# Three chunks of a retention kernel turned by transposing DMAs from ScalarE's queue instead of TensorE's and SyncE's

## The chip, the cores and the metric

One core of a Trainium2 chip. The time is the device time of one execution in microseconds; several runs are summed up by their median. All times inside an execution are counted from its first instruction.

## The reference

Two layers. The first is retention (attention with a decay in place of a softmax) on `q`, `k`, `v` of shape 8 x 8 x 576 x 64 (batch, heads, sequence, head size); its output, 4608 x 512, goes through a gated feed-forward layer.

```
scores = q @ k.T / sqrt(64)
gamma  = 1 - 2 ** (-5 - head)
ret    = scores * (gamma ** (i - j) where i >= j, else 0)
x      = (ret @ v), heads side by side        # 4608 x 512
out    = (sigmoid(x @ w_gate) * (x @ w_val)) @ w_out    # 512 -> 1536 -> 512
```

## The kernel before

The sequence of a batch is cut into chunks of 128 tokens. Inside a chunk the scores are computed in full; between chunks a running state per head (the sum of k times v) is carried. The decay is split into factors for q and for k, so that a cast to bf16 and a multiplication by a table are one operation. The first chunks are done in pairs at the start (`PAIRS`); the other thirty, called "later chunks" here and numbered 0 to 29 in the list `STEPS`, are done while the feed-forward layer of earlier tokens runs. The feed-forward layer takes tokens in blocks (`BLOCKS`): block 0 of the main loop has 256 tokens and begins at token 512, then one more of 256, then blocks of 512.

For a later chunk s there are these steps:

- `load(s)`: three loads from HBM (`k_s`, `q_s`, `v_s`), given out on SP's queue (L171);
- `cast_qk`: k and q times their tables into `natural_qk[s]` (`qk` in the profile, L429), on GpSimd, for chunks 0 and 1 q on VectorE; `cast_v` (L444);
- the turning: `T` holds q and k with the head size on the partitions. Either `turn_step(s)` does it by eight TensorE transposes into PSUM (L630) and one copy each by ScalarE and VectorE (L632), for the chunks in `TURNED`, or `cross(s)` does it by one transposing DMA from SBUF to SBUF (L448), given out on SP's queue right behind the casts;
- `slot_of_two`: scores (`row`, L686) that read `T`, products for the state (`new`, L695), the mask (L704) and the values (`val`, L718 and L734).

`casts_to(s)` does the loads, casts and `cross` of all chunks up to s that are still to be done; its loads run one or two chunks ahead of its casts.

In block 0 of the main loop `h_units` goes through twelve units on TensorE, alternately `h_g` (gate, two columns of 128 out of 1536) and `h_v` (value). Each fills one of three PSUM banks that rotate (`ffn_psum`). ScalarE takes `h_g` out by a sigmoid into `gv` (L889), VectorE multiplies `h_v` into it (L891). The table `SUMS_AT` says what further work is written behind which unit: an entry such as `0.6:t01p` stands for block 0, unit 6, `turn_step(1)`, `0.0:c03p` for `casts_to(3)`. The scores of chunks 0 and 1 stand behind unit 10, those of chunks 2 and 3 in the next slot. Every engine runs its instructions in the order in which they are written.

Just ahead of the main loop the first 512 tokens go through the output matmul, `op_first` (L1549): `FIRST_OP_CUTS` counts how many of its 512-wide matmuls are split into two of 256.

The completion of a DMA is counted by one of eight counters, `DMAHW0` to `DMAHW7`, that are handed out in turn. A DMA waits until the one that had its counter before it has landed.

Of the kernel before, what the change touches and what calls it, by code (L numbers as in the profile page):

```python
# [16 lines left out]
def kernel(  # L17
# [19 lines left out]
    nc = tc.nc  # L37
# [109 lines left out]
    def half(x):  # L147
        return slice(x * 64, x * 64 + 64)
# [169 lines left out]
    def wo_sums(i, part, parts, eng=nc.vector):  # L318

        fp = slice(part * (NFC // 2) // parts, (part + 1) * (NFC // 2) // parts)  # L320
        b11, b12, b21, b22 = (wo_sb[:, r::2, c:c + DM // 2][:, fp] for r in range(2) for c in (0, DM // 2))
        t1, t2, t4 = (wt_sb[:, j, fp] for j in range(3))
        to, a, b = ((t1, b12, b11), (t2, b22, t1), (b12, b22, b12), (t4, b21, t2))[i]
        eng.tensor_tensor(out=to, in0=a, in1=b, op=ALU.subtract)
# [34 lines left out]
    def w_sums(kind, i, u, eng):  # L359

        a11, a12, a21, a22 = w_quarters(kind, u)
        s1, s2, s4 = (wt3_sb[kind][j][u] for j in range(3))
        to, a, b, op = ((s1, a21, a22, ALU.add), (s2, s1, a11, ALU.subtract), (seventh(kind, u), a11, a21, ALU.subtract),
                        (s4, a12, s2, ALU.subtract))[i]
        eng.tensor_tensor(out=to, in0=a, in1=b, op=op)
# [54 lines left out]
    def cast_qk(s, i, eng):  # L420
        c = STEPS[s][1]
        if i == 1:
            natural_qk[s] = nat_pool.tile([P, 2, M, P], BF16, tag="qk", name=f"qk_{s}")
        to = natural_qk[s][:, i].rearrange("p m (y d) -> p y m d", y=2)
        if i == 1 and s >= SCALED_V:
            (on_pool if s in K_ON_POOL else on_act)(out=to, in_=by_halves(loaded[s][0]))
            return
        tab = (qtab, ktab)[i][:, c, :].rearrange("p (y m) -> p y m", y=2).unsqueeze(3).to_broadcast([P, 2, M, D])
        eng.tensor_tensor(out=to, in0=by_halves(loaded[s][1 - i]), in1=tab, op=ALU.mult)  # L429
# [8 lines left out]
    def cast_v(s, eng):  # L438
        natural["v", s] = nat_pool.tile([P, H, D], BF16, tag="v", name=f"v_{s}", bufs=6)
        if s >= SCALED_V:  # L440
            tab = ktab[:, STEPS[s][1], :].unsqueeze(2).to_broadcast([P, H, D])
            nc.gpsimd.tensor_tensor(out=natural["v", s], in0=loaded[s][2], in1=tab, op=ALU.mult)  # L442
        else:
            eng(out=natural["v", s], in_=loaded[s][2])  # L444

    def cross(s):
        t = att_pool.tile([P, 2, M, P], BF16, tag="T", name=f"T_{s}", bufs=6)
        nc.sync.dma_start_transpose(out=t.rearrange("p j m t -> p (j m) t"),  # L448
                                    in_=natural_qk[s].rearrange("p j m d -> p (j m d)"))
        turned[s] = t  # L450

# [167 lines left out]
            cols = slice(t0, t0 + P)  # L619
            eng(out=x_out(slice(i * k, (i + 1) * k), cols), in_=x_in(ps[:, at_m:at_m + k], cols))  # L620

    TURNED = (0, 1, 7)

    def turn_step(s):

        t = att_pool.tile([P, 2, M, P], BF16, tag="T", name=f"T_{s}", bufs=6)
        for i, ((pool, tag), eng) in enumerate(zip(VALS, (on_act, on_dve))):
            ps = pool.tile([P, M, P], BF16, tag=tag, name=f"turn_{s}_{i}")
            for m in range(M):
                nc.tensor.matmul(ps[:, m, :], lhsT=natural_qk[s][:, i, m, :], rhs=ident, is_transpose=True,  # L630
                                 start=(m == 0), stop=(m == M - 1))
            eng(out=t[:, i], in_=ps)  # L632
        turned[s] = t
# [6 lines left out]
    def new_state(key, dt=BF16):  # L640
        b, c, j = key
        if dt == BF16 and c == LAST - 1 and j == NJ - 1:
            return nat_pool.tile([P, M, D], dt, tag="sf", name=f"sf_{b}_{c}_{j}", bufs=5)
        tag, bufs = ("s32", 3) if dt == FP32 else ("sb", 4)
        if (tag, b, c) not in both_steps:
            both_steps[tag, b, c] = nat_pool.tile([P, NJ, M, D], dt, tag=tag, name=f"{tag}_{b}_{c}", bufs=bufs)
        return both_steps[tag, b, c][:, j]
# [142 lines left out]
    def after_two(vals, news, i, late, first, closes):  # L790

        if i == 0 and not news:
            for s in vals:
                inter(s, [(1,), (0,)])
        if i < NJ:
            if len(vals) == 2 and at_col[vals[1]] == at_col[vals[0]] + P:
                leave_two(vals, i)
            else:
                for s in vals:
                    nc.scalar.copy(out=x_out(ALL, cols_of(s, i)), in_=x_in(val_ps[s][i], cols_of(s, i)))  # L800
        if i == NJ:
            for s in vals:
                if dealt(cols_of(s, 0)):
                    x_sums(at_col[s], X_LATE if late and closes else X_FIRST)
        if late and news and i == (NJ if closes else NJ - 1):
            casts_to(min(done["cast"], news[-1] + LEAD_CAST + 1) if first and not closes else news[-1] + LEAD_CAST + 1)
        for n, s in enumerate(news):
            b, c = STEPS[s]
            if c == LAST:
                continue  # L810
            if i == n:
                add_state(s, 0)
                add_state(s, 1)
                if s < 2 * len(PAIRS_AT) and s == max(x for x in news if STEPS[x][1] < LAST):
                    ffn_psum.free_last(ffn_psum.held.pop())
            if i == n + 1:
                keep_both(b, c, [j for j in range(NJ) if totals.pop((s, j), None) is not None], on_act)
# [16 lines left out]
    def first_batch_state():  # L834

        whole = new_state((0, LAST - 1, NJ - 1))
        for hh in range(2):
            for y in range(2):
                (nc.vector.tensor_copy if hh == y else nc.sync.dma_start)(
                    out=whole[half(y), hh::2, :], in_=sbd[3][half(hh), 2 * y:2 * y + 2, half(hh)])  # L840
        state[0, LAST - 1, NJ - 1] = whole
# [6 lines left out]
    def loads_to(s):  # L848
        while done["ld"] <= min(NS - 1, s):
            load(done["ld"])  # L850
            done["ld"] += 1

    def casts_to(s):
        while done["cast"] <= min(NS - 1, s):
            x = done["cast"]
            loads_to(x + (AHEAD[x] if x < len(AHEAD) else 2))
            cast_qk(x, 1, nc.gpsimd)
            cast_qk(x, 0, nc.vector if x < 2 else nc.gpsimd)
            if x not in TURNED:
                cross(x)  # L860
            cast_v(x, on_dve if x == 0 else on_act if x in V_ON_ACT else on_pool)
            done["cast"] += 1
# [6 lines left out]
    def next_two(vals, news, late, first, closes):  # L869
        slot_of_two(vals, news)  # L870
        if news and not late:
            casts_to(news[-1] + 2)
        for i in range(3):
            pending.append(lambda i=i: after_two(vals, news, i, late, first, closes))
# [661 lines left out]
    for i in (0, 1, 3):  # L1536
        w_sums("g", i, 1, nc.vector)

    FIRST_OP_CUTS = 20
    op_cut = []  # L1540

    def op_first(fcs, nbs, opps):
        for fc in fcs:
            for nb in nbs:
                parts = 2 if fc and len(op_cut) < FIRST_OP_CUTS else 1
                op_cut.extend([fc] * (parts - 1))
# [27 lines left out]
    keep_state((1, 0, 1), st_tiles[1], on_act)  # L1574
    op_first((5, 6, 7, 8, 9), range(3), opps)
    casts_to(0)
    third_intra([PV, QK[0]])
    pair_st(2, 1)
# [15 lines left out]
    store(opps[3], 3 * P, on_act)  # L1594
    casts_to(1)

    SUMS_AT = ("0.0:c03p 0.1:f00p 0.3:g00p 0.3:w10v 0.3:w11v 0.6:t01p 0.7:o10p 0.8:c02v "
# [4 lines left out]
    sums_at = {}  # L1602
    for x in SUMS_AT:
        at, x = x.split(":")
        u, i, eng = int(x[1]), int(x[2]), nc.gpsimd if x[3] == "p" else nc.vector
        sums_at.setdefault(tuple(int(y) for y in at.split(".")), []).append(
            lambda k=x[0], u=u, i=i, eng=eng: wo_sums(i, u, 3, eng) if k == "o" else
            casts_to(10 * u + i) if k == "c" else turn_step(i) if k == "t" else first_batch_state() if k == "f" else
            w_sums(k, i, u, eng))
    PAIRS_AT = ((0, 10), (0, 11), (1, 10), (1, 0))  # L1610
    paired = 0
# [80 lines left out]
```

## Time and profile before

| | us |
|---|---|
| median of three runs | 304.57 |
| lowest and highest of them | 303.11, 306.47 |
| the profiled execution, in all | 303.89 |
| its span, first to last instruction | 302.2 |
| TensorE busy | 295.6 |
| VectorE, GpSimd, ScalarE busy | 230.4, 225.8, 204.9 |
| transposing DMAs on SP's queue | 27 |

The span is what the views of the profile count in; the total has 1.7 us more around it. In the views PE is TensorE, PEld its weight loads, DVE VectorE, ACT ScalarE, POOL GpSimd, SPq SyncE's queue of DMAs and ACTq ScalarE's. A row of the order of time has its start, its length, the engine, the line, the operation, output and inputs; in brackets the idle time ahead of it and what ended it. Matmul rows in a group overlap, so their spacing is read from the starts.

### The profile page before, as it was taken

What the parts mean: (1) busy time and instruction counts of PE and PEld (TensorE: products, weight loads), DVE (VectorE), ACT (ScalarE), POOL (GpSimd) and SP (SyncE); (2) the same over time, 40 slices, a digit from 0 to 9 for tenths busy, and PEclk for the clock granted to TensorE, in tenths of its full rate; (3) what the DMA queues carried; (4) which work ended last, traced back from release to release, by engine and by line L of the source; (5) the groups of instructions that cost most, each with busy time, mean ns of one, the idle gap of its engine ahead of it and who ended that gap; (6) DMA issues with size and microseconds to landing.
All of it is one profiled execution on the core that took longest, in us unless ns stands there. A gap on an engine that the chain in (4) does not pass through costs nothing.

```text
span 302.2 us, 10696 instructions
## 1 busy us (share of the span) xinstructions
PE 295.6 (98%) x4437; PEld 250.0 (83%) x4437; DVE 230.4 (76%) x439; ACT 204.9 (68%) x414; POOL 225.8 (75%) x253
## 2 busy tenths in 40 slices
PE   7999999999999999999999999999999999999994
PEld 3677876978868888888888888888888888888883
DVE  5967895796986998789748974896489848935893
ACT  6755565335369657985798589857985698559830
POOL 5775854846669888978997898789978946860780
PEclk9999999999999999999999999999999999999999
DMA  7999999979998989999749967976694165004013
GB/s 205 336 370 379 322 334 229 210 160 202 213 175 184 257 173 196 219 201 262 141 108 199 259 143 155 218 185 143 124 204 132 37 123 193 4 2 139 3 36 104
DMA packets 146464, 54.99 MB, mean 182 GB/s; under 512 B 124400, under 2 KB 139760, under 8 KB 146416
## 3 DMA queue, kind: packets, MB, share of 16 engines
q1 hardware_dynamic: 145328, 53.59, 73.6%
q8 instruction: 34, 0.56, 0.8%
q10 hardware_dynamic: 1088, 0.72, 0.8%
q14 instruction: 14, 0.11, 0.1%
HBM read 37.75 MB, written 9.44 MB: 156 GB/s over the span
## 4 chain that ended last, share of the span: by engine, by line
PE 92%; DVE 2%; DMA 2%; issue 1%; ACT 1%; POOL 0%; SPq 0%; DVEq 0%
PE gatea L1046 12%; PE wa L1046 11%; PE qa L1173 11%; PE qe L1173 9%; PE gatee L1046 6%; PE we L1046 5%; PE op L1549 4%; PE h_v L886 3%; PE h_g L886 3%; PE gateg L1046 3%; PE wg L1046 3%; PE hv L1374 3%; PE op L1306 3%; PE val L718 2%; PE qa L1249 2%; PE hg L1374 2%
## 5 line engine op out<-in xcount | busy, mean ns | idle before, releaser
L1046 PEld LDWEIGHTS <-wg_sb 128*128 128x128 bf16 x348 | 34.1, 98 | 4.1
L1073 POOL TENSOR_TENSOR gv<-gv,wu 128x512 bf16<-128x512 bf16 x20 | 23.5, 1174 | 15.5 <-DVE wu L1085 15.4
L1173 PEld LDWEIGHTS <-gsum 128*128 128x128 bf16 x312 | 30.0, 98 | 3.7
L429 POOL TENSOR_TENSOR qk<-q,qtab 128x512 bf16<-128x512 f32 x28 | 30.3, 1082 | 3.5 <-DMA q<-in_q_dram 3.5
L1046 PEld LDWEIGHTS <-wv_sb 128*128 128x128 bf16 x296 | 28.9, 98 | 3.6 <-issue 0.2
L1085 DVE TENSOR_TENSOR gu<-gatee,gu 128x512 f32<-128x512 f32 x22 | 15.2, 690 | 19.4 <-ACT gateg L1077 10.2
L943 POOL TENSOR_TENSOR gsum<-gsum,gv 128x256 bf16<-128x256 bf16 (+1 forms) x20 | 17.6, 890 | 14.4 <-DVE gsum L943 12.6
L1046 PEld LDWEIGHTS <-wgt_sb 128*128 128x128 bf16 x264 | 25.8, 98 | 3.0
L1046 PE MATMUL gatea<-xsum,wg_sb 128*128 128x256 bf16 x172 | 25.6, 273 | 0.0
L1173 PEld LDWEIGHTS <-gv 128*128 128x128 bf16 x228 | 21.8, 98 | 2.7
L1088 DVE TENSOR_TENSOR gs<-gatea,gs 128x512 f32<-128x512 f32 x22 | 15.2, 689 | 9.5 <-PE gatea L1046 9.4
L943 POOL TENSOR_TENSOR gsum<-gv,gsum 128x256 bf16<-128x256 bf16 (+1 forms) x24 | 21.9, 922 | 0.2
L429 POOL TENSOR_TENSOR qk<-k,ktab 128x512 bf16<-128x512 f32 x11 | 11.6, 1054 | 13.4 <-DMA k<-in_k_dram 13.2
L704 DVE TENSOR_TENSOR pt<-row,tri 128x512 bf16<-128x512 f32 x30 | 19.2, 680 | 2.8 <-PE row L686 2.6
L442 POOL TENSOR_TENSOR v<-v,ktab 128x512 bf16<-128x512 f32 x19 | 20.9, 1101 | 0.0
L1046 PE MATMUL wa<-xsum,wv_sb 128*128 128x256 bf16 x136 | 20.4, 273 | 0.1
L658 ACT CAST sb<-s 128x512 bf16<-128x512 f32 (+1 forms) x26 | 14.3, 569 | 8.8 <-DVE s L829 8.7
L788 ACT CAST xT<-val 128x512 bf16<-128x512 f32 x26 | 14.7, 592 | 7.0 <-PE val L734 7.0
L943 DVE TENSOR_TENSOR gsum<-gv 128x512 bf16<-128x512 bf16 (+1 forms) x34 | 19.1, 589 | 0.0
L1046 PEld LDWEIGHTS <-wvt 128*128 128x128 bf16 x168 | 16.4, 98 | 1.9
L943 POOL TENSOR_TENSOR gsum<-gv 128x256 bf16<-128x256 bf16 (+1 forms) x20 | 17.6, 882 | 0.0
L1071 ACT ACTIVATE gv<-gs 128x512 bf16<-128x512 f32 x22 | 13.9, 633 | 5.4 <-DVE gs L1088 5.4
(210 smaller groups left out, 883.9 us busy)
## 6 DMA issues: line engine op xcount, KB each, us to landing
k<-in_k_dram SPq DMA_DIRECT2D x26, 256.0 KB, 3.9
q<-in_q_dram SPq DMA_DIRECT2D x26, 256.0 KB, 4.2
v<-in_v_dram SPq DMA_DIRECT2D x26, 256.0 KB, 4.6
out_dram<-ob SPq DMA_DIRECT2D x24, 256.0 KB, 2.7
wg<-in_moe_w_gate_dram SPq DMA_DIRECT2D x12, 256.0 KB, 5.4
wv<-in_moe_w_val_dram SPq DMA_DIRECT2D x12, 256.0 KB, 5.6
wo<-in_moe_w_out_dram SPq DMA_DIRECT2D x12, 256.0 KB, 5.6
v32p<-in_v_dram SPq DMA_DIRECT2D x6, 256.0 KB, 4.5
```

Of the source, the lines that this page charges most:

```text
L429: eng.tensor_tensor(out=to, in0=by_halves(loaded[s][1 - i]), in1=tab, op=ALU.mult)
L442: nc.gpsimd.tensor_tensor(out=natural["v", s], in0=loaded[s][2], in1=tab, op=ALU.mult)
L704: nc.vector.tensor_tensor(out=t[:, y, 0:n].rearrange("p i m t -> p (i m) t"), in0=rows_tile[ss[0]][y][:, 0:n].rearrange("p i m t -> p (i m ...
L788: nc.scalar.copy(out=to, in_=src)
L886: nc.tensor.matmul(ps[:, i], lhsT=w_sb[:, kc, (fc + i) * P:(fc + i + 1) * P], rhs=xT(kc, slice(t0, t0 + n)), start=(kc == 0), stop=(kc == ...
L943: eng.tensor_tensor(out=to, in0=a, in1=b, op=op)
L1046: nc.tensor.matmul(ps[:, f], lhsT=w[:, kc, f * P:(f + 1) * P], rhs=x[:, kc], start=(first and f == 0 and kc == 0), stop=(f == 1 and kc == ...
L1073: eng.tensor_tensor(out=to, in0=to, in1=src[:, part], op=ALU.mult)
L1085: nc.vector.tensor_tensor(out=me["u2"], in0=e, in1=me["u2"], op=ALU.add)
L1088: nc.vector.tensor_tensor(out=me["s5"], in0=a, in1=me["s5"], op=ALU.add)
L1173: nc.tensor.matmul(ps[:, b], lhsT=left(fp)[:, b * P:(b + 1) * P], rhs=right(fp), start=(first and fp == 0 and b == 0), stop=(fp == NFC // ...
L1374: nc.tensor.matmul(ps[:, cols], lhsT=(wg_sb if what == "g" else wv_sb)[:, kc, fc * P:(fc + 1) * P], rhs=xT(kc, cols), start=(kc == 0), sto ...
```

## The change

Chunk 1 is no longer turned on TensorE: `TURNED` loses it. Chunks 1, 2 and 3 are turned by `cross` on ScalarE's queue, and `casts_to` leaves their `cross` out. Three new entries of `SUMS_AT` place them: chunk 1 behind unit 0 of block 0, chunk 2 behind unit 2, chunk 3 behind unit 7. `FIRST_OP_CUTS` goes from 20 to 28, so eight more of the output matmuls ahead of the loop are split. TensorE's number of instructions stays 8876. From `cross` on, line numbers are higher by two in the changed kernel.

```diff
+    ON_ACT = (1, 2, 3)
+
-    def cross(s):
+    def cross(s, queue=nc.sync):
         t = att_pool.tile([P, 2, M, P], BF16, tag="T", name=f"T_{s}", bufs=6)
-        nc.sync.dma_start_transpose(out=t.rearrange("p j m t -> p (j m) t"),
+        queue.dma_start_transpose(out=t.rearrange("p j m t -> p (j m) t"),
                                     in_=natural_qk[s].rearrange("p j m d -> p (j m d)"))
...
-    TURNED = (0, 1, 7)
+    TURNED = (0, 7,)
...
-            if x not in TURNED:
+            if x not in TURNED + ON_ACT:
                 cross(x)
...
-    FIRST_OP_CUTS = 20
+    FIRST_OP_CUTS = 28
...
-    SUMS_AT = ("0.0:c03p 0.1:f00p 0.3:g00p 0.3:w10v 0.3:w11v 0.6:t01p 0.7:o10p 0.8:c02v "
+    SUMS_AT = ("0.0:c03p 0.1:f00p 0.2:x02p 0.3:g00p 0.3:w10v 0.3:w11v 0.0:x01p 0.7:x03p 0.7:o10p 0.8:c02v "
...
-            casts_to(10 * u + i) if k == "c" else turn_step(i) if k == "t" else first_batch_state() if k == "f" else
+            casts_to(10 * u + i) if k == "c" else turn_step(i) if k == "t" else cross(i, nc.scalar) if k == "x" else first_batch_state() if k == "f" else
```

ScalarE in block 0 of the main loop, before: the sigmoids of units h_g_0 to h_g_10 and the copy of the turned chunk 1. What a row waits for stands in brackets, by the engine or the DMA counter.

```order
63 L889 ACTIVATE gv_0_1164<-h_g_0_1165 128x2x256 [waits PE_49]
64 L889 ACTIVATE gv_0_1164<-h_g_2_1210 128x2x256 [waits PE_49]
65 L889 ACTIVATE gv_1_1233<-h_g_4_1234 128x2x256 [waits PE_49]
66 L889 ACTIVATE gv_1_1233<-h_g_6_1254 128x2x256 [waits PE_49]
67 L632 COPY T_1264<-turn_0_1265 128x512 [waits PE_49]
68 L889 ACTIVATE gv_2_1288<-h_g_8_1289 128x2x256 [waits PE_49]
```

The same place now; `qk_1167`, `qk_1183` and `qk_1194` are the casts of chunks 1, 2 and 3.

```order
63 L891 ACTIVATE gv_0_1172<-h_g_0_1173 128x2x256 [waits PE_49]
64 L450 DMA_TRANSPOSE T_1199<-qk_1167 128x8x128 [waits DMAHW7_49,DVE_49,Pool_49]
65 L891 ACTIVATE gv_0_1172<-h_g_2_1216 128x2x256 [waits PE_49]
66 L450 DMA_TRANSPOSE T_1226<-qk_1183 128x8x128 [waits DMAHW2_49,Pool_49]
67 L891 ACTIVATE gv_1_1241<-h_g_4_1242 128x2x256 [waits PE_49]
68 L891 ACTIVATE gv_1_1241<-h_g_6_1262 128x2x256 [waits PE_49]
69 L450 DMA_TRANSPOSE T_1282<-qk_1194 128x8x128 [waits DMAHW3_49,Pool_49]
70 L891 ACTIVATE gv_2_1285<-h_g_8_1286 128x2x256 [waits PE_49]
```

Three transposes have come between the sigmoids, each with a wait on a DMA counter and on GpSimd, and the copy has gone.

SP's queue, before, from chunk 2's q load to chunk 4's transpose; a load's counter is the one that it waits for.

```order
62 L171 DMA q_2_1035<-in_q_dram 128x8x64 [waits DMAHW7_49,Pool_49]
63 L171 DMA v_2_1037<-in_v_dram 128x8x64 [waits DMAHW0_49,Pool_49]
64 L171 DMA k_3_1153<-in_k_dram 128x8x64 [waits DMAHW1_49,Pool_49]
65 L171 DMA q_3_1155<-in_q_dram 128x8x64 [waits DMAHW2_49,DVE_49]
66 L171 DMA v_3_1157<-in_v_dram 128x8x64 [waits DMAHW3_49,Activation_49]
67 L448 DMA_TRANSPOSE T_1178<-qk_1175 128x8x128 [waits DMAHW4_49,PE_49,Pool_49]
68 L171 DMA k_4_1182<-in_k_dram 128x8x64 [waits DMAHW5_49]
69 L171 DMA q_4_1184<-in_q_dram 128x8x64 [waits DMAHW6_49]
70 L171 DMA v_4_1186<-in_v_dram 128x8x64 [waits DMAHW7_49,Activation_49]
71 L448 DMA_TRANSPOSE T_1191<-qk_1188 128x8x128 [waits DMAHW0_49,PE_49,Pool_49]
```

And now, from chunk 3's q load on.

```order
65 L171 DMA q_3_1163<-in_q_dram 128x8x64 [waits DMAHW2_49,DVE_49]
66 L171 DMA v_3_1165<-in_v_dram 128x8x64 [waits DMAHW3_49,Activation_49]
67 L171 DMA k_4_1188<-in_k_dram 128x8x64 [waits DMAHW4_49]
68 L171 DMA q_4_1190<-in_q_dram 128x8x64 [waits DMAHW5_49]
69 L171 DMA v_4_1192<-in_v_dram 128x8x64 [waits DMAHW6_49,Activation_49]
70 L841 DMA sf_3_1_1211<-sbd_265 64x2x64 [waits DMAHW0_49]
71 L841 DMA sf_3_1_1211<-sbd_265 64x2x64 [waits DMAHW1_49]
72 L450 DMA_TRANSPOSE T_1401<-qk_1398 128x8x128 [waits DMAHW3_49,DMAHW2_49,DMAHW4_49,DVE_49,DMAHW7_49,PE_49,Pool_49]
```

The transposes of chunks 2 and 3 have left SP; chunk 4's transpose (the last row) now waits for all three on ScalarE's queue as well (counters 7, 2 and 3).

TensorE behind h_g_6, now; before, eight pairs of LDWEIGHTS and MATMUL of `turn_0` and `turn_1` stood between the second and the third row.

```order
1311 L888 LDWEIGHTS wg_sb
1312 L888 MATMUL h_g_6_1262<-xT_1110,wg_sb 128x256
1313 L888 LDWEIGHTS wv_sb
1314 L888 MATMUL h_v_6_1272<-xT_1110,wv_sb 128x256 [waits Activation_49]
1315 L888 LDWEIGHTS wv_sb
```

h_v_6 now follows h_g_6 at once; its wait for ScalarE (the sigmoid of h_g_4) was there before too.

## The prediction

> **What bounds the kernel now.** I read the page first: shares of the engines, the 40 slices, the chain that ended last; then the list of waits.
>
> ```profile
> span 302.2 us, 10696 instructions
> PE 295.6 (98%) x4437; PEld 250.0 (83%) x4437; DVE 230.4 (76%) x439; ACT 204.9 (68%) x414; POOL 225.8 (75%) x253
> ...
> PE   7999999999999999999999999999999999999994
> ...
> PEclk9999999999999999999999999999999999999999
> ...
> PE 92%; DVE 2%; DMA 2%; issue 1%; ACT 1%; POOL 0%; SPq 0%; DVEq 0%
> ```
> ```profile
> PE idle L242 <- DVE blank L229: 1.1, 1, 1.1
> ```
>
> TensorE is busy in every slice but the first and last, at full granted clock, and holds 92% of the chain. Its longest wait for another engine is 1.1 us, at the very start. So two things alone can move the end: TensorE's own work, and a wait that it does not have today. Any such wait stays in the total, since no later idle time is there to swallow it.
>
> The change sits between 50 and 70 us. The windows of that stretch, TensorE's busy time first after the length:
>
> ```profile
> 50.00:60.00 10.00, 10.00 (x97) 8.64 (x96) 7.38 (x13) 4.64 (x10) 6.91 (x8) 1.00 0.97 216
> 60.00:70.00 10.00, 9.93 (x257) 7.89 (x255) 8.68 (x18) 4.36 (x10) 4.48 (x6) 1.00 0.86 187
> ```
>
> TensorE is full there, ScalarE under half busy; the 16 DMA engines are at 0.97 and 0.86. Then the order of time on TensorE (start, length) and on ScalarE:
>
> ```profile
> 54.83 1.04 PE L886 MATMUL h_g<-xT,wg_sb 128*128 128x256 bf16 x8
> 55.70 1.04 PE L886 MATMUL h_v<-xT,wv_sb 128*128 128x256 bf16 x8
> 56.58 1.04 PE L886 MATMUL h_g<-xT,wg_sb 128*128 128x256 bf16 x8
> 57.45 0.61 PE L630 MATMUL turn<-ident,qk 128*128 128x128 bf16 x8
> 57.90 1.04 PE L886 MATMUL h_v<-xT,wv_sb 128*128 128x256 bf16 x8
> ...
> 61.48 0.45 PE L686 MATMUL row<-T 64*64 64x64 bf16 x32
> ...
> 62.13 0.28 PE L886 MATMUL h_v<-xT,wv_sb 128*128 128x256 bf16 x1
> ```
> ```profile
> 54.16 0.60 ACT L889 ACTIVATE gv<-h_g 128x512 bf16<-128x512 f32 x1 [1.15 <-PE h_g L886]
> 55.91 0.60 ACT L889 ACTIVATE gv<-h_g 128x512 bf16<-128x512 f32 x1 [1.15 <-PE h_g L886]
> 57.65 0.60 ACT L889 ACTIVATE gv<-h_g 128x512 bf16<-128x512 f32 x1 [1.15 <-PE h_g L886]
> 58.15 0.58 ACT L632 COPY T<-turn 128x512 bf16<-128x512 bf16 x1
> ```
>
> By the program's order these are h_g_4, h_v_4, h_g_6, the turning of chunk 1, h_v_6, h_g_8 on TensorE, and the sigmoids of h_g_2, h_g_4 and h_g_6 on ScalarE. A unit takes 55.70 − 54.83 = 0.87. The units rotate through three PSUM banks, so a unit needs the bank of three units earlier: h_v_6 needs the sigmoid of h_g_4 (the wait on Activation in its row above). Today that sigmoid ends at 56.51, 1.4 us before h_v_6 begins.
>
> **What goes.** The eight transposes of chunk 1 leave TensorE: 57.90 − 57.45 = **−0.45**. The ScalarE and VectorE copies that went with them lie beside full TensorE work: 0. SP loses two transposes and so gives out chunk 4's loads some 1.8 us earlier; TensorE waits for none of them: 0.
>
> **The split matmuls.** Eight 512-wide matmuls become sixteen 256-wide ones. Rows for both widths:
>
> ```profile
> 46.99 3.20 PE L1549 MATMUL op<-wo_sb,gv 128*128 128x512 bf16 x14
> ...
> 50.03 0.61 PE L630 MATMUL turn<-ident,qk 128*128 128x128 bf16 x8
> ```
> ```profile
> L886 PEld LDWEIGHTS <-wv_sb 128*128 128x128 bf16 x48 | 4.6, 98 | 0.5
> ```
>
> Fourteen of 512 take 50.03 − 46.99 = 3.04, 0.217 each; two of 256 take 2 × 0.87/8 = 0.218. Eight splits cost 0.01. If the extra weight loads (98 ns) were not hidden it would be 8 × 0.098 = 0.8; the 256-wide units run at 0.109 with the same loads, so they are hidden. I take **0**.
>
> **What comes.** Three transposes stand in ScalarE's queue, each between two sigmoids. What is queued behind a waiting one waits too. When may each start? The first waits for counter DMAHW7, the second for DMAHW2; in SP's rows above these counters belong to q_2 and q_3, chunk 2's and chunk 3's q loads. SP's own times, then issue to landing of those two loads (from the starts of the rows), then of all 27 transposes:
>
> ```profile
> 49.11 0.85 SPq L171 DMA_DIRECT2D q<-in_q_dram  x1
> ...
> 52.35 1.90 SPq L171 DMA_DIRECT2D q<-in_q_dram  x1
> 54.35 1.08 SPq L171 DMA_DIRECT2D v<-in_v_dram  x1
> 55.53 1.70 SPq L448 DMA_TRANSPOSE T<-qk  x1
> 57.29 0.57 SPq L171 DMA_DIRECT2D k<-in_k_dram  x1
> ...
> 59.98 1.88 SPq L448 DMA_TRANSPOSE T<-qk  x1
> ```
> ```profile
> DMA to landing us min/median/max: 4.3/4.3/4.3
> ```
> ```profile
> DMA to landing us min/median/max: 4.9/4.9/4.9
> ```
> ```profile
> L448 SPq DMA_TRANSPOSE T<-qk x27: 1232/1697/4111, 55.5 to 244.0; - x27
> ...
> DMA to landing us min/median/max: 2.7/4.2/6.1
> ```
>
> q_2 lands at 49.11 + 4.3 = 53.41, q_3 at 52.35 + 4.9 = 57.25. How long giving out a transpose holds ScalarE no row shows; on SP it holds 1.23 to 4.11, median 1.70. The only loads on ScalarE's queue near by are two of half the size:
>
> ```profile
> 0.81 0.49 ACTq L186 DMA_DIRECT2D k32p<-in_k_dram  x1
> ```
> ```profile
> 0.81 0.47 SPq L186 DMA_DIRECT2D k32p<-in_k_dram  x1
> ```
>
> So the bounds are 0.49 and 4.11; I take 1.70, the median and the row of this very stretch (55.53).
>
> Step by step: the first transpose goes at 53.41 and frees ScalarE at 55.11; the sigmoid of h_g_2 ends at 55.71 instead of 54.76, which h_v_4 (55.70) barely sees. The second goes at 57.25, frees ScalarE at 58.95; the sigmoid of h_g_4 ends at 59.55. With the turning gone h_v_6 could start at 57.45, so TensorE stands for **+2.10**. Behind it VectorE's product of h_v_4:
>
> ```profile
> 57.63 0.68 DVE L891 TENSOR_TENSOR gv<-gv,h_v 128x512 bf16<-128x512 bf16 x1
> ```
>
> 59.55 + 0.68 = 60.23, before h_g_8 wants the bank at 59.55 + 0.87 = 60.42: no second stop. The third waits for GpSimd's q cast of chunk 3:
>
> ```profile
> 57.39 1.22 POOL L429 TENSOR_TENSOR qk<-q,qtab 128x512 bf16<-128x512 f32 x1
> ```
>
> That ends at 58.61, behind the sigmoid of h_g_6 by then (60.05); it holds to 61.75, and the sigmoid of h_g_8 ends at 62.35, where h_v_10, now 62.13 + 1.65 = 63.78, needs it: no stop. Are the turned chunks in time? Chunk 1 lands near 53.41 + 4.2 = 57.6, read at 61.48 + 1.65. Chunk 3 lands at 60.05 + 4.2 = 64.3, read in the second group of rows:
>
> ```profile
> 66.47 0.44 PE L686 MATMUL row<-T 64*64 64x64 bf16 x32
> ```
>
> that is 68.1 then. Chunk 4's transpose on SP now also waits for these three, 64.3 instead of 63.60, and chunk 5's behind it slips by the same 0.7. Today:
>
> ```profile
> 73.39 1.52 SPq L448 DMA_TRANSPOSE T<-qk  x1
> ```
> ```profile
> DMA to landing us min/median/max: 5.1/5.1/5.1
> ```
> ```profile
> 80.02 0.54 PE L686 MATMUL row<-T 64*64 64x64 bf16 x31
> ```
>
> 78.5 against 80.0; TensorE is by then 1.65 later, so the margin grows.
>
> **The sum:** −0.45 + 0 + 2.10 = **+1.65**. The profiled execution took 303.89 in all (span 302.2 and 1.7 around it), giving 305.5. The median of the three runs is 304.57, 0.68 above it; a median is asked for, so I give 306.2. With the hold at 0.49: 57.25 + 0.49 + 0.60 = 58.34, +0.44. With 4.11: 61.96, +4.06. If q_3 lands a microsecond later, since the first transpose now moves beside it (a load or a transpose is some 1 us of DMA time: v_3 is given out 2 us after q_3 and the next thing 1.2 after that), add up to 1.0.
>
> **Rivals.** *A, ScalarE lets go at once, or the wait on q_3 is over early.* A gap of 1.15 us stands before each sigmoid, so a hold of about a microsecond that starts when q_2's cast is done would fit. Without the wait on q_3 the second transpose goes at 55.6, the sigmoid of h_g_4 ends at 57.9, and h_v_6 starts where it does today: 0. With a short hold as well, all of −0.45 is kept. With the wait, no better than +0.44. So −0.45 to +0.44, 304.1 to 305.0. Against it: the wait stands in ScalarE's row. It decides at 57.45: whichever ends the sigmoid of h_g_4 before that pays nothing.
>
> *B, both queues get in each other's way.* SP gives out loads without a gap from 52.35 on, and some rows there last 1.90 where others last 0.57. If ScalarE's transposes take turns with them, the second starts up to a load (1.08) later and holds up to 4.11: +2.7 to +4.1, 307.3 to 308.7. Against it: at 0.81 us both queues gave out a load side by side in 0.47 and 0.49. [...]
>
> [...]
>
> That the change is not what it says is ruled out: the rows above have the three transposes on ScalarE.
>
> **How the numbers follow.** Main case 0.55 (305.7 to 306.9: from a hold of 1.23, the shortest on SP, to the 1.88 of 59.98 with q_3 half a microsecond late), A 0.22, B 0.18, C 0.05. A measurement of this kernel tells about 1%, 3.05 us, from no change. Slower by more: C, a little over half of B, and 0.05 of the main case, 0.21. Faster by more would need six times what is removed: 0.03. The rest, 0.76, is within 1%. The range leaves out C and what noise adds at the ends: 303.8 (A, less 0.3 for runs that spread from 303.11 to 306.47) to 308.6 (B).
>
> **What the changed profile would show.** ScalarE's queue with three transposes near 53.4, 57.3 and 60; a wait of TensorE of 1.6 to 2.9 at h_v_6, released by the sigmoid; no turning at 57.45; later groups of rows shifted by one constant, with no new wait. I am wrong if TensorE has no wait there (A), or if it stands elsewhere: on the turned chunk 1 or 3, or on SP behind chunk 4's transpose.

## The result, and the profile after

The changed kernel took 306.22 us (median of 20 runs, 303.98 to 307.98); the kernel before, measured beside it, 303.75 (20 runs, 302.98 to 306.47). The ratio is 1.0074, 95% interval 1.0049 to 1.0098: some 2.2 us slower (the medians are 2.5 apart), less than the 1% that was taken as the limit. The ratios, here and below, are estimated from all runs that were not slow as a whole, and so are not quite those of the medians. A second measurement of the same kernel (e10 below) gave 1.0041, 1.0019 to 1.0062. The two together put the cost near 1.7 us.

The profiled execution took 306.09 in all, against 303.89 for the one before. Its page, the same lines as those of before: span and instructions, the engines' busy time, the chain that ended last by engine.

```profile
span 304.2 us, 10690 instructions
...
PE 295.4 (97%) x4431; PEld 250.7 (82%) x4437; DVE 231.3 (76%) x438; ACT 204.3 (67%) x413; POOL 225.5 (74%) x253
...
PE 82%; DMA 7%; DVE 5%; POOL 2%; ACT 2%; issue 1%; ACTq 0%; SPq 0%; POOLq 0%; DVEq 0%
```

TensorE is as busy as before (295.4 against 295.6) in a span that is 2.0 longer: it waits where it did not. Its share of the chain has dropped from 92% to 82%, but that alone shows little: in further profiles without the change it is 88% (e12) and 84% (e5). The list of waits (total, times, longest) names the first place:

```profile
PE h_v L888 <- ACT gv L891: 1.2, 2, 0.7
PE idle L242 <- DVE blank L229: 1.1, 1, 1.1
PE gateg L1048 <- ACT gateg L1079: 0.5, 1, 0.5
```

The first and the third line are new. TensorE in order of time, from h_g_4 to h_g_8:

```profile
54.80 1.04 PE L888 MATMUL h_g<-xT,wg_sb 128*128 128x256 bf16 x8
56.25 1.03 PE L888 MATMUL h_v<-xT,wv_sb 128*128 128x256 bf16 x8 [0.42 <-ACT gv L891]
57.12 1.04 PE L888 MATMUL h_g<-xT,wg_sb 128*128 128x256 bf16 x8
58.90 1.03 PE L888 MATMUL h_v<-xT,wv_sb 128*128 128x256 bf16 x8 [0.74 <-ACT gv L891]
59.77 1.04 PE L888 MATMUL h_g<-xT,wg_sb 128*128 128x256 bf16 x8
```

A unit takes 0.87, so h_v_4 is late by 56.25 − 54.80 − 0.87 = 0.58 and h_v_6 by 58.90 − 57.12 − 0.87 = 0.91 (the brackets show less, since they count from the modelled end of the matmul before). ScalarE in the same stretch:

```profile
54.22 1.34 ACTq L450 DMA_TRANSPOSE T<-qk  x1
55.60 0.60 ACT L891 ACTIVATE gv<-h_g 128x512 bf16<-128x512 f32 x1 [2.63 <-POOL qk L429]
56.96 1.25 ACTq L450 DMA_TRANSPOSE T<-qk  x1
58.25 1.09 ACT L891 ACTIVATE gv<-h_g 128x512 bf16<-128x512 f32 x2 [2.05 <-PE h_g L888]
59.60 1.26 ACTq L450 DMA_TRANSPOSE T<-qk  x1
60.92 0.60 ACT L891 ACTIVATE gv<-h_g 128x512 bf16<-128x512 f32 x1 [1.58 <-PE h_g L888]
```

The sigmoid of h_g_2 ends at 56.20, that of h_g_4 at 58.85; h_v_4 and h_v_6 start 0.05 behind them. The bracket of the first sigmoid names GpSimd, but its cast was done long before; SP's queue shows what ended the wait. Below stand its loads of q_2, q_3 and v_3 (the k load behind them and chunk 4's transpose are read further down), and then the times to landing of these three loads.

```profile
48.23 0.80 SPq L171 DMA_DIRECT2D q<-in_q_dram  x1
...
51.82 2.14 SPq L171 DMA_DIRECT2D q<-in_q_dram  x1
54.05 0.88 SPq L171 DMA_DIRECT2D v<-in_v_dram  x1
54.98 0.84 SPq L171 DMA_DIRECT2D k<-in_k_dram  x1
...
64.62 1.35 SPq L450 DMA_TRANSPOSE T<-qk  x1
```
```profile
DMA to landing us min/median/max: 5.9/5.9/5.9
```
```profile
DMA to landing us min/median/max: 5.1/5.1/5.1
```
```profile
DMA to landing us min/median/max: 5.5/5.5/5.5
```

q_2 lands at 54.1, q_3 at 56.9, v_3 at 59.5: the three transposes start at 54.22, 56.96 and 59.60, each within 0.1 of the landing whose counter it reuses. None of them needs these data: chunk 2's last cast was done at 55.2, before the second transpose could go.

Against the profile of before TensorE is at −0.04 ahead of h_v_4, at +0.55 there and at +1.00 at h_v_6: −0.45 for the turning, +0.58 and +0.91 for the stops. At the end it is at +1.6. Half a microsecond of the rest comes at 182.92, where ScalarE stood for a k load, with TensorE's row and ScalarE's:

```profile
182.92 0.60 PE L1048 MATMUL gateg<-xT,wg_sb 128*128 128x256 bf16 x4 [0.47 <-ACT gateg L1079]
```
```profile
181.46 0.62 ACT L426 CAST qk<-k 128x512 bf16<-128x512 f32 x1 [1.05 <-DMA k<-in_k_dram]
```

### The profile page after: what moved, and what is told of

Same layout as the page of the kernel before. It is cut to its first block, busy times and chain, and to the rows that moved or that the text cites. A ratio compares the mean times of both kernels' runs of the same rounds, so it can differ in the third digit from the quotient of the medians.

```text
span 304.2 us, 10690 instructions
## 1 busy us (share of the span) xinstructions
PE 295.4 (97%) x4431; PEld 250.7 (82%) x4437; DVE 231.3 (76%) x438; ACT 204.3 (67%) x413; POOL 225.5 (74%) x253
## 4 chain that ended last, share of the span: by engine, by line
PE 82%; DMA 7%; DVE 5%; POOL 2%; ACT 2%; issue 1%; ACTq 0%; SPq 0%; POOLq 0%; DVEq 0%
PE gatea L1048 12%; PE wa L1048 11%; PE qa L1175 9%; PE qe L1175 7%; PE gatee L1048 6%; PE we L1048 6%; DMA k<-in_k_dram 6%; PE gateg L1048 3%; PE wg L1048 3%; PE op L1308 3%; PE h_v L888 2%; PE h_g L888 2%; PE qa L1251 2%; PE hg L1376 2%; PE hv L1376 2%; PE idle L242 2%
## 5 line engine op out<-in xcount | busy, mean ns | idle before, releaser
L1048 PEld LDWEIGHTS <-wg_sb 128*128 128x128 bf16 x348 | 34.0, 98 | 4.8 <-issue 0.7
L1048 PEld LDWEIGHTS <-wv_sb 128*128 128x128 bf16 x296 | 29.0, 98 | 3.4
L1048 PEld LDWEIGHTS <-wgt_sb 128*128 128x128 bf16 x264 | 25.8, 98 | 3.0
L1048 PE MATMUL gatea<-xsum,wg_sb 128*128 128x256 bf16 x172 | 25.6, 273 | 0.0
L1090 DVE TENSOR_TENSOR gs<-gatea,gs 128x512 f32<-128x512 f32 x22 | 15.2, 689 | 8.9 <-PE gatea L1048 8.8
L1048 PE MATMUL wa<-xsum,wv_sb 128*128 128x256 bf16 x136 | 20.4, 273 | 0.0
L1048 PEld LDWEIGHTS <-wvt 128*128 128x128 bf16 x168 | 16.4, 98 | 1.9
L1073 ACT ACTIVATE gv<-gu 128x512 bf16<-128x512 f32 x22 | 14.1, 640 | 5.1 <-DVE gu L1087 5.1
```

Of the source, the lines that this page charges most:

```text
L1048: nc.tensor.matmul(ps[:, f], lhsT=w[:, kc, f * P:(f + 1) * P], rhs=x[:, kc], start=(first and f == 0 and kc == 0), stop=(f == 1 and kc == ...
L1073: nc.scalar.activation(out=to, in_=src[:, part], func=AF.Sigmoid)
L1090: nc.vector.tensor_tensor(out=me["s5"], in0=a, in1=me["s5"], op=ALU.add)
```

## The experiments

The ratios are to the kernel before, run beside each group (e1 to e4: 304.17 us, e5 to e8: 303.51, e9 to e12: 303.29). "Stop" is the lateness of h_v_4 plus h_v_6 in the profile, from starts as above.

| | edit | us, runs | ratio (95%) | stop |
|---|---|---|---|---|
| after | the change | 306.22, 20 | 1.0074 (1.0049 to 1.0098) | 1.49 |
| e10 | the change again | 304.43, 11 | 1.0041 (1.0019 to 1.0062) | 1.25 |
| e4 | the change, 20 cuts | 307.88, 6 | 1.0124 (1.0088 to 1.0160) | 1.63 |
| e11 | e4 again | 305.25, 9 | 1.0067 (1.0042 to 1.0091) | 2.27 |
| e2 | another counter | 306.02, 12 | 1.0063 (1.0035 to 1.0090) | 0.58 |
| e1 | behind the next sigmoid | 305.14, 12 | 1.0031 (1.0009 to 1.0052) | 0 |
| e6 | places with slack | 303.98, 12 | 1.0016 (0.9993 to 1.0038) | 0 |
| e9 | e6, 20 cuts | 305.08, 12 | 1.0057 (1.0030 to 1.0083) | 0.2 |
| e8 | chunks 2 and 3 alone | 303.92, 12 | 1.0007 (0.9992 to 1.0022) | 0.1 |
| e7 | chunk 1 alone | 304.83, 11 | 1.0044 (1.0015 to 1.0072) | 0 |
| e3 | on SyncE's queue | 305.62, 12 | 1.0043 (1.0018 to 1.0068) | 0 |
| e5 | before, 28 cuts | 304.47, 12 | 1.0016 (0.9995 to 1.0037) | 0 |
| e12 | before again | 303.50, 12 | 1.0005 (0.9987 to 1.0022) | 0 |

The times do not follow the last column line by line: e1, e2, e3, e7 and e9 have other waits, which are told with each.

### e10 and e12: both kernels again

No edit.

> The changed kernel once more, unaltered, for a second profile. If the stops at h_v_4 and h_v_6 belong to the change they come again, 0.9 to 2 us together, since the first transpose waits for q_2 and the second for q_3, whose landings move by a microsecond from run to run. If the late step near 181 us belongs to it too, TensorE waits there again by 0.4 to 0.6; if it is chance, it is gone or elsewhere. Ratio to before 1.005 to 1.010.

> The kernel before, unaltered, against itself: shows how far the comparison and a single profile stray with nothing changed. Expected: ratio 1.000 within 0.2%, TensorE's rows near 58 us within 1.7 us of the first profile of before, since the start of the program alone has moved them by -0.9 to +1.7 in the profiles so far; no wait at h_v.

ScalarE and TensorE in e10:

```profile
53.40 1.35 ACTq L450 DMA_TRANSPOSE T<-qk  x1
54.79 0.60 ACT L891 ACTIVATE gv<-h_g 128x512 bf16<-128x512 f32 x1 [2.10 <-PE h_v L888]
56.42 1.25 ACTq L450 DMA_TRANSPOSE T<-qk  x1
```
```profile
56.31 1.04 PE L888 MATMUL h_g<-xT,wg_sb 128*128 128x256 bf16 x8
58.37 1.03 PE L888 MATMUL h_v<-xT,wv_sb 128*128 128x256 bf16 x8 [1.02 <-ACT gv L891]
```

The stop at h_v_6 came again: 58.37 − 56.31 − 0.87 = 1.19. At h_v_4 only 0.06 is left, because the first transpose starts 0.8 earlier (at 53.40, not at 54.22). Near 181 us TensorE does not wait at all in e10, nor in e4 and e11; e1 (0.54) and e9 (0.32) have that wait, the profiles without the change have not. So it is not a fixed part of the change, but whether the change makes it likelier is open. The ratio is just under the expected 1.005. Against the first profile of before TensorE loses 0.81 from 41.9 us to h_v_6 (−0.34 there, +0.47 here), the 1.25 less the 0.45 of the turning; it ends level with it all the same, because that profile of before has small waits, 0.35 of them near 66 us, that e10 lacks. Before against itself gives 1.0005, and its second profile is within 0.45 of the first throughout; but e5's, of the same program up to 44 us, is already 1.7 later at 38 us. So the comparison resolves about 0.2%, and a step of half a microsecond that stands in one profile alone is not laid to the change.

### e1, e2 and e6: the same transposes at other places

e1 writes each one behind a later sigmoid. To change the counters e1 and e2 also move the copies of the first state (`f00p`) to unit 12; e2 leaves the places as they are, and its second transpose reuses v_2's counter instead of q_3's. e6 keeps the copies and takes places where the sigmoid behind has slack.

```diff
-    0.0:x01p 0.2:x02p 0.7:x03p 0.1:f00p
+    0.2:x01p 0.5:x02p 0.8:x03p 0.12:f00p    # e1
+    0.0:x01p 0.2:x02p 0.7:x03p 0.12:f00p    # e2
+    0.2:x01p 0.7:x02p 0.8:x03p 0.1:f00p     # e6
```

> The three transposes stay on ScalarE's queue, but each stands one place later: behind the sigmoids of h_g_2, h_g_4 and h_g_8 instead of those of h_g_0, h_g_2 and h_g_6; the state copy first_batch_state is written behind unit 12, so that the counters that they wait for belong to q_2, v_2 and k_3. Theory (the loss is TensorE standing at h_v_4 and h_v_6 for sigmoids that are queued behind transposes): no wait there over 0.2 us, h_v_10 begins 0.45 earlier than in the kernel before, time 0.998 to 1.000 of before. Rival (the transposes on a second queue cost by themselves, through DMA traffic or the shifted instructions of the engines): 1.004 to 1.010 of before, as the changed kernel.

> Places on ScalarE as in the changed kernel; only first_batch_state is written behind unit 12, by which the second transpose waits for the counter of v_2 (landed at about 55) instead of q_3 (about 57), the third for k_3. Theory (the wait for q_3's landing makes the larger of the two stops): the second transpose starts right behind the first one's hold, about 55.6, the stop at h_v_6 falls from 0.9 to under 0.3 us, the one at h_v_4 (0.6, from q_2's landing and the hold) stays; time 0.6 to 0.9 us below the changed kernel, about 1.003 to 1.006 of before. Rival (the holds of 1.3 us alone do it, whatever they wait for): both stops stay, 1.0074.

> The changed kernel with the three transposes at other places: chunk 1 behind the sigmoid of h_g_2, chunk 2 behind that of h_g_6, chunk 3 behind that of h_g_8; the copies of the first state stay where they are in the changed kernel. The counters waited for are then those of k_3, q_3 and v_3. Theory W: the first starts near 55.5 and lets go near 56.8, so the sigmoid of h_g_4 ends by 57.4 and h_v_6 starts at 57.45 (0.45 earlier than before); the second starts behind the sigmoid of h_g_6 near 58.3, the third near 60.2; no stop of TensorE at h_v_4, h_v_6, h_v_10, and none at the values of chunk 0 and 1 at 66 us. Ratio 0.9985, 303.7 where before has 304.2. Rival T (late chunks): chunk 1 lands at 60.5 to 61 and chunk 3 near 65, so a stop of up to 1 us at the scores of chunks 0 and 1 or 2 and 3: ratio 1.000 to 1.003. Rival L (the late load near 181 us comes with the change): no stop there, but +0.6 near 181, net +0.2, ratio 1.0005.

In e2 the second transpose goes at 55.01 instead of 56.96:

```profile
53.54 1.34 ACTq L450 DMA_TRANSPOSE T<-qk  x1
...
55.01 1.89 ACTq L450 DMA_TRANSPOSE T<-qk  x1
```

The stop falls from 1.49 to 0.58 (0.29 at each unit): what is left is the first transpose's wait on q_2 and two holds. The time, 306.02, did not fall by the 0.6 to 0.9 that was expected. The profile has two waits of TensorE that the change has not: 0.5 at the values (L736), as for the moved copies in e1 below, and 1.0 for VectorE (L1048 behind L1090), whose cause was not followed. In e1 both stops are gone, but the moved copies stood on VectorE ahead of the sums of the state, and the values of chunks 0 and 1 waited for them (VectorE, then TensorE):

```profile
65.02 1.12 DVE L841 COPY sf<-sbd 64x128 bf16<-64x128 bf16 x2
```
```profile
67.40 0.25 PE L736 MATMUL val<-T,sb 64*64 64x64 bf16 x6 [1.12 <-ACT sb L660]
```

That is a fault of e1's edit, not of the transposes, and e6 removes it. In e6 the transposes stand at

```profile
53.75 1.34 ACTq L450 DMA_TRANSPOSE T<-qk  x1
55.39 0.60 ACT L891 ACTIVATE gv<-h_g 128x512 bf16<-128x512 f32 x1 [1.15 <-PE h_g L888]
57.13 0.60 ACT L891 ACTIVATE gv<-h_g 128x512 bf16<-128x512 f32 x1 [1.15 <-PE h_g L888]
57.20 1.25 ACTq L450 DMA_TRANSPOSE T<-qk  x1
58.88 0.60 ACT L891 ACTIVATE gv<-h_g 128x512 bf16<-128x512 f32 x1 [1.15 <-PE h_g L888]
58.94 1.27 ACTq L450 DMA_TRANSPOSE T<-qk  x1
```

where every sigmoid keeps its old gap of 1.15. TensorE goes through without a stop and h_v_6 follows h_g_6 after a plain unit:

```profile
56.06 1.04 PE L888 MATMUL h_g<-xT,wg_sb 128*128 128x256 bf16 x8
56.94 1.04 PE L888 MATMUL h_v<-xT,wv_sb 128*128 128x256 bf16 x8
```

The stop is therefore made by where the transposes stand, with the counters that come with the place, and not by giving them out on ScalarE. The time is that of before (1.0016); the 0.45 saved (0.15%) is below what these runs resolve.

### e7 and e8: parts of the change

```diff
-    ON_ACT = (1, 2, 3)      0.0:c03p ... 0.0:x01p 0.2:x02p 0.7:x03p
+    ON_ACT = (1,)           0.0:x01p 0.0:c03p                        # e7, TURNED (0, 7), 28 cuts
+    ON_ACT = (2, 3)         0.0:c03p 0.2:x02p 0.6:t01p 0.7:x03p      # e8, TURNED (0, 1, 7), 20 cuts
```

> The changed kernel with chunk 1 alone on ScalarE's queue, written behind unit 0 ahead of the casts of chunks 2 and 3, and chunks 2 and 3 back on SyncE's queue. Its counter is that of q_1, landed long before. Theory W: the transpose starts right behind the sigmoid of h_g_0 near 53.0 and lets go near 54.3, ahead of the sigmoid of h_g_2: no stop at h_v_4 or h_v_6, and TensorE keeps 0.45 from h_v_6 on; ratio 0.9985. Rival T: chunk 2's transpose on SyncE now waits until chunk 1 has landed (near 58.5) instead of starting at 55.5, chunk 3's follows near 61 and lands near 65.5, so the scores of chunks 2 and 3 at 66 us see a stop of 0 to 1 us: ratio 0.9985 to 1.002.

> The kernel before with chunks 2 and 3 alone moved to ScalarE's queue, at the changed kernel's places (behind units 2 and 7); chunk 1 stays on TensorE, 20 cuts as before. The counters are those of k_3 and q_3. Theory W: k_3 lands near 55.5, the first of the two lets go near 56.8, the sigmoid of h_g_4 ends near 57.4, and h_v_6 behind the turning wants it at 57.9: no stop, ratio 1.000. Rival Q (what costs is that transposes are given out on ScalarE at all, by the holds or by the traffic): a stop of 0.5 to 1 at h_v_4 or h_v_6 as in the changed kernel, ratio 1.002 to 1.004. Rival S (placement in the program): slower by 0.5% as with 20 cuts and all three moved, 305.7.

e8 costs nothing. Without chunk 1's transpose the counters shift: chunk 2's waits for k_3 and starts at 55.08, and the sigmoid of h_g_4 is out at 57.07, in time for h_v_6 at 57.12.

```profile
55.08 1.34 ACTq L450 DMA_TRANSPOSE T<-qk  x1
56.47 1.08 ACT L891 ACTIVATE gv<-h_g 128x512 bf16<-128x512 f32 x2 [2.59 <-POOL qk L429]
```

But here the turning still stands ahead of h_v_6; without its 0.45 the same sigmoid would have been half a microsecond late. So e8 alone does not clear the holds; e6, with three of them and without the turning, does. e7 has no stop at the units either, but the rival's at the scores of chunks 2 and 3. SP's queue, then TensorE:

```profile
53.25 1.56 SPq L171 DMA_DIRECT2D v<-in_v_dram  x1
58.19 1.36 SPq L450 DMA_TRANSPOSE T<-qk  x1
...
61.94 3.36 SPq L450 DMA_TRANSPOSE T<-qk  x1
```
```profile
67.47 0.32 PE L688 MATMUL row<-T 64*64 64x64 bf16 x16 [1.03 <-DMA T<-qk]
```

SP stands from 54.8 to 58.19, until ScalarE's transpose (given out at 52.17) has landed, 5.9 later; all its loads behind that wait too (the next goes at 59.61). That wait costs SP's queue 3.4 us. Its 1.0044 is more than the rival's 1.002: the profile has two more waits of TensorE, 0.36 at 66.06 and 0.6 for VectorE (L1048 behind L1027), whose cause was not followed.

### e3: the same places, on SyncE's queue

```diff
-    cross(i, nc.scalar) if k == "x"
+    cross(i, nc.sync) if k == "x"
```

> The changed kernel with the three transposes given out on SyncE's queue at the same places of the program, so chunk 1 is off TensorE and ScalarE has none of them. Theory: no stop at h_v_4 and h_v_6, h_v_10 some 0.45 earlier than before, 0.998 to 1.000 of before. Rival (what costs is chunk 1's crossbar transpose itself, 0.25 MB more through the DMA engines, or the order of the loads): slower than before by 0.3% or more.

The profiled execution took 309.59, 4 us above the median, so only the place of the wait is read from it:

```profile
66.07 0.32 PE L688 MATMUL row<-T 64*64 64x64 bf16 x16 [2.40 <-DMA T<-qk]
```
```profile
61.96 2.04 SPq L450 DMA_TRANSPOSE T<-qk  x1
```

On SP chunk 1's transpose stands behind the loads up to chunk 4, goes at 61.96 and lands too late for its scores. The sigmoids are free, and the time (1.0043) is that of the change's second measurement: one stop for another.

### e4, e5, e9 and e11: the number of split matmuls

e4 and e11 are the change, e9 is e6, each with 20 cuts; e5 is before with 28.

```diff
-    FIRST_OP_CUTS = 28
+    FIRST_OP_CUTS = 20
```

> The changed kernel with FIRST_OP_CUTS at 20, as before the change: eight matmuls of 512 whole again, sixteen instructions fewer on TensorE. Theory (a split costs nothing): 1.005 to 1.010 of before, as the changed kernel. Rival (the splits cost up to 0.8 us, or shift where TensorE's instructions are fetched): 0.3% or more away from the changed kernel.

> The kernel before with one edit: 28 instead of 20 of the output matmuls ahead of the main loop are split; chunk 1 stays on TensorE, chunks 2 and 3 on SyncE's queue. Theory W (all that the change costs is what stands ahead of ScalarE's sigmoids): ratio to before 1.000 within 0.2%, TensorE's row h_v_6 at 57.9 as before, within the 0.5 us by which the start of the program varies. Rival S (the split itself, or where it puts the later instructions in the program, has a price or a gain): with the transposes in place 20 cuts were 0.5% slower than 28, so here 28 should be some 1.5 us faster than before, 302.7 where before has 304.2. Rival L (a k load that lands late near 181 us is chance): a step of some 0.6 us near 181 us may or may not appear here, where nothing has been moved.

> The changed kernel with the transposes behind the sigmoids of h_g_2, h_g_6 and h_g_8 and with 20 cuts in place of 28. Theory W (the turning gone, nothing in the way): TensorE 0.45 earlier from h_v_6 on and no stop; ratio 0.9985, some 0.45 us under before. Theory J (single runs vary by 1 to 3 us with when the loads land, so 0.45 is not to be seen): ratio between 0.998 and 1.002. Rival S (20 cuts with all three transposes on ScalarE's queue put the program into a slower place): ratio 1.005 or more, as the changed kernel with 20 cuts had 1.0124.

> The changed kernel with 20 cuts once more. Theory J (few runs, loads that land late): with twice the runs the ratio comes down to that of the changed kernel, 1.005 to 1.009. Rival S (the number of split matmuls has a price of its own here): 1.010 to 1.014 again, and the profile shows a stop outside of the block 50 to 65 us that the changed kernel does not have.

About half of e4's 1.0124 did not come again: repeated it is 1.0067. But 20 cuts came out slower in all three pairs (e4 and e11 against the change, e9 against e6, by 0.3 to 0.5%), though only e11 and e10 were run side by side, and their intervals overlap. With 28 cuts TensorE has 8876 instructions, as before, since the eight splits put back the 16 that the turning took; with 20 it has 8860. All three profiles with 8860 (of two kernels, since e4 and e11 are the same) show an idle time of TensorE at the same matmul that nothing in the trace explains. In e4, e11 and e9:

```profile
233.96 0.25 PE L736 MATMUL val<-T,sb 64*64 64x64 bf16 x7 [0.64 <-issue]
```
```profile
233.56 0.25 PE L736 MATMUL val<-T,sb 64*64 64x64 bf16 x7 [0.46 <-issue]
```
```profile
235.34 0.25 PE L736 MATMUL val<-T,sb 64*64 64x64 bf16 x7 [0.17 <-issue]
```

None of the kernels with 8876 has one there, nor has e5 with 8892. But the profile of the change has one of 0.29 at a matmul of this line at 176.58, and e10, the same kernel, has none: such idle times also come and go. That the number of instructions makes them is a guess that was not tried, and at 0.17 to 0.64 they are less than the 0.8 to 1.5 us by which 20 cuts came out slower. e9 shows a second thing: its third transpose goes at 60.83, takes 6.1 to land, and SP gives out chunk 4's only at 67.10 (64.62 in the change). ScalarE, SP, and the two stops of TensorE behind it:

```profile
60.83 2.31 ACTq L450 DMA_TRANSPOSE T<-qk  x1
```
```profile
67.10 1.36 SPq L450 DMA_TRANSPOSE T<-qk  x1
```
```profile
80.17 1.03 PE L888 MATMUL h_g<-xT,wg_sb 128*128 128x256 bf16 x8 [0.68 <-DVE gv L893]
...
87.76 0.45 PE L688 MATMUL row<-T 64*64 64x64 bf16 x32 [0.60 <-DMA T<-qk]
```

This execution took 308.21, 3 us above e9's median. The second row is a transposed chunk that came too late. At the first TensorE waits for VectorE's product (0.68). GpSimd had stood 8.73 for a k load behind that transpose, given out at 68.56, and cast it from 73.21. That the late load is the cause of the first stop was not shown.

## Why the prediction was right, and where not

**The time.** 306.2 was forecast and 306.22 measured, but that is closer than the working deserves: that is luck. The three runs of before were 0.8 above the 303.75 of the next twenty, and the rise of 1.65 stands between the 2.2 and the 1.2 of the two measurements. The stops less the turning explain 1.0 and 0.8 of these; what the rest consists of is only in part known.

**The turning, −0.45.** Held: in e6, without a stop, h_v_6 starts 0.88 behind h_g_6 instead of 1.32.

**The splits, 0.** Held for their matmuls: in e5 TensorE is 1.66 behind the profile of before at 38.26, ahead of the split matmuls, and 1.67 at h_v_6, behind them; its ratio of 1.0016 is no change that can be told. Why 28 cuts came out better than 20 once the turning is gone was not foreseen and is open.

**The stop at h_v_6, +2.10.** The mechanism held in four profiles. In after, e10, e4 and e11 the second transpose goes at 56.96, 56.42, 57.69 and 58.15 (in after 0.04 behind q_3's landing at 56.92), and h_v_6 starts at 58.90, 58.37, 59.63 and 60.16, 1.94 to 2.01 behind it each time. e2 cuts the stop down by another counter, and e6 takes it away by another place. The size was off, above all in the term of the hold: 1.25 instead of 1.70. With q_3 0.33 earlier than forecast, h_v_6 came 1.49 later than it could have without any stop, not 2.10. Of these 1.49 TensorE spent 0.58 at h_v_4 and 0.91 at h_v_6, so the wait at h_v_6 itself stayed under the 1.6 to 2.9 that the changed profile was to show.

**"Barely sees" at h_v_4.** This step failed. It set the sigmoid's end at 55.71 against a need at 55.70, no margin at all, behind a transpose that starts between 53.35 and 55.68 in the four profiles. In after q_2 landed at 54.1 and not at 53.41, and the stop was 0.58 even with the shorter hold (1.57 in e11, 0.06 in e10, none in e4). It cost the sum nothing: what h_v_4 loses, h_v_6 no longer has to wait, since the second transpose goes when q_3 lands. Over the four profiles the two stops together are 1.25 to 2.27, mean 1.66, so the block costs 1.2 net of the turning, not 1.65.

**The third transpose.** No stop, as forecast, but it waited for v_3's counter (59.5), not for GpSimd's cast. The two earlier transposes were checked against their counters, this one was not.

**Landing and SP's queue.** Chunk 1 was to land at 57.6, 4.2 after a start at 53.4; it was given out at 54.22 and took 5.5. Its scores come late enough (62.48) that nothing waited. Chunk 4's transpose was forecast at 64.3 and came at 64.62. That the margin behind it grows was too simple: in e9 the loads of later chunks came late behind this wait (it ended at 67.10), and in e7 behind one of the same kind (58.19).

**"One constant, no new wait".** Not so: the profile after has a wait of 0.47 near 183 us. e10 has none there, so it is no fixed price.

**The rivals.** A is out: in after the first two transposes start 0.09 and 0.04 behind the landings of q_2 and q_3, and in all four profiles with these places the second holds the sigmoid of h_g_4 back until 0.04 or 0.05 before h_v_6 starts. B's price was also worked out too low: a start later by 1.08 and a hold of 4.11 together would be +5.1, not +4.1. On ScalarE B is not seen in the change: the first transpose held it 1.34 from 54.22 while SP gave out two loads, at 54.05 in 0.88 and at 54.98 in 0.84, and e6's third held it 1.27 from 58.94 while SP gave out nothing from 58.98 on. Neither queue waits for the other in these rows. Elsewhere it stays open: beside the third transpose SP took 1.75 from 59.42 for a copy of the state that takes 0.73 before the change, and in e4 the first transpose held ScalarE 2.04 from 53.35; but SP has rows as long where ScalarE gives out nothing (2.14 from 51.82). C, a clock that falls behind a pause (0.05 of the chances), is a term that no run shows: the mean granted clock was 0.994 to 1.0 in the profiled executions; 0.994 is e3's, which has the longest wait of TensorE in the lists, 2.40.

## What to carry to other kernels

A DMA on a computing engine's queue cost that engine two things here, the wait for its operands and its counter (1.24 us ahead of the first transpose in the profile after, from 52.98 to 54.22) and the time of giving it out (1.3 us); what stood behind it needed that much slack. Where the counter belonged to a load on another queue, the slack had to cover the spread of the start too (56.42 to 58.15 for the second transpose in four profiles). Look for the place where the next instruction of the engine is needed last: moved by one to five units the same three transposes cost nothing that could be measured (1.0016 in e6; with 20 cuts, in e9, it was 1.0057). The saving of 0.15% on TensorE was to be seen in e6's profile (0.45 at h_v_6) and not in its time.

## What was not expected of the hardware

Giving out a transpose held ScalarE 1.25 to 1.37 us in most cases, and never over 2.31 (e9), where SP's holds range from 1.23 to 4.11 before the change. Landing took 5.5, 5.3 and 4.6 from ScalarE in the profile after, 5.9 in e7 and 6.1 for the third in e9, where SP had 2.7 to 6.1 before, with a median of 4.2. And with 16 instructions fewer on TensorE an idle time of 0.17 to 0.64 us stood some 180 us later, at the same instruction in three of three profiles; the cause is not known.
